# A sum of the first chunk's inverse on GpSimd, a copy on ScalarE, and a new order of all steps

## The chip, the core and the metric

The kernel runs on one core of one Trainium2 chip. A core has five engines with a queue each: TensorE (PE; its weight loads are shown as PEld), VectorE (DVE), ScalarE (ACT), GpSimd (POOL) and SyncE (SP, which here issues nearly all DMAs). Each works through its own queue in order and waits at semaphores for the others. The metric is the device time of one execution in microseconds (us), lower is better; it is given as the median of several executions.

## The reference

All is float32, but the two weights arrive as float64. First a linear recurrence with a 40x40 state for each of 4 x 8 heads over 768 time steps, then a two-layer perceptron on the 3072 tokens:

```python
for t in range(S):
    y[:, :, t] = np.einsum('bhd,bhde->bhe', rt, state)
    Sa = np.einsum('bhde,bhe->bhd', state, at)
    state_decay = state * wt[:, :, None, :] - np.einsum('bhd,bhe->bhde', Sa, bt)
    state = state_decay + np.einsum('bhd,bhe->bhde', vt, kt)
...
x = np.ascontiguousarray(attn_out.transpose(0, 2, 1, 3)).reshape(B * S, H * D)
h = x @ w_in
g = 0.5 * h * (1.0 + erf(h * inv_sqrt2))
return (g @ w_out).astype(np.float32)
```

Here B, H, S, D are 4, 8, 768, 40; `w_in` is 320x2048 and `w_out` 2048x320.

## The kernel before

The sequence is cut into 12 chunks of 64 steps. Within a chunk the recurrence becomes matrix products and the inverse of a triangular 64x64 matrix per head, which is built from 32x32 blocks; the chunks follow one another through the state. Behind each chunk its 256 tokens go through the perceptron, 8 steps `mh` for the first product, 4 `ge` for the activation, and for chunks 1 to 11 seven products `m1` to `m7` for the second (the first chunk uses four plain steps `pm`).

The program is a list of small functions, the steps. `order` (lines 19 to 111) returns one long string of tokens such as `mh.0.3`; line 1436 performs them in that order, and each step puts its instructions at the end of its engines' queues. No scheduler changes it: the order of the tokens is the order of every queue, and waits follow from who wrote and read which memory. The first number of a token is the chunk, or for the `c` steps a unit of the weights.

The steps that matter here:

- `sb` (L785) and `sk` (L790) scale b and k by the decays; `ta`, `tb`, `tk`, `tv`, `tr` (L752, L194) transpose on PE for chunks 0 to 2; `nm` and `nk` (L194, L865) give the triangular matrix N, `am`/`ak` and `vm`/`vk` two more such products.
- The inverse of chunk 0 goes by squaring: `qt` (L1001) transposes N, `qi` (L1008) adds the identity to N, `qi.0` for partitions 0 to 63 and `qi.1` for 64 to 127; a last letter `p` puts it on GpSimd, `v` on VectorE. `qm.0` to `qm.4` are the products on PE, `qz`, `qb`, `qa`, `qc`, `ql`, `qx` the work between them, `jm`, `jc`, `km`, `kt0`, `kt1` the last block.
- The inverses of chunks 1 to 11 go row by row on GpSimd: `iz`, then `ic.c.j0.j1` (L962, L964), 62 small instructions for a chunk. They need `nx` (L928) on VectorE, which needs `nd` (L923) on ScalarE and `nk`. `wx` (L933) takes the result.
- `av`, `xm` and the copies `xc0`, `xc1` (L1155) bring products into SBUF; `sm` applies the inverse, `sc` (L1176) masks; `pk` and `pb` give state and output, `om` and `od` scale them, `ox` moves parts of the output between partitions by eleven DMAs for each chunk, `ym` and `tn` use the turned state.
- The weights are loaded as raw words of float64 in 18 units (`Lf`, `Lf5` for `w_in`, units 0 to 9; `Ls` for `w_out`, units 10 to 17) and made into float32 by `cp`, `ce`, `cm`, `cs` (L607, L614, L621, L628) and then one of three ends: `cv` on VectorE (L636, L637), `cl`/`cn` on ScalarE with `cg` on GpSimd (L659, L660), or `cx` on PE with `cy`. The raw words lie in memory that later work needs: those of units 10 to 13 in `w_out_sb` itself, those of unit 15 in `gt`, the activations' tile, those of units 14 and 17 one after the other in `bk_rows`.
- `warm` are matmuls without use for the result. `parity_set` (a transpose on VectorE) reads what `stripes_set` on GpSimd wrote; `warm_first` needs `warm_set` on VectorE; `wT` and `cu` need `sums_mask` on GpSimd.
- PSUM is four banks. `take` (line 177) gives out the bank that has been free longest, `drop` returns it, both in the order of the tokens, so a product waits for the last reader of what lay in its bank.
- At the end `so.11.0` and four `sz` write the last rows; the last letter names the queue, `a` ScalarE's, `s` SP's.

Of the kernel before, what the change touches and what calls it, by code (L numbers as in the profile page):

```python
# [18 lines left out]
def order(chunks, first_seven):  # L19
    return """  # L20
        Lw.0 of_half_set warm_set pads_a.1 warm_first pads_a.0 stripes_set Lw.1 bias_set pads_rows.1 pads_VR.1
        sums_mask pads_w.0 pads_extra.3 La.0 pads_VR.0 identity pads_extra.0 first_ones.0 Lf.0.0.0 pads_w.1
# [8 lines left out]
        Lf5.0.1 ic.1.12.16 cp.7 ce.7 av.0 qa.4 cm.2 qx Ls.0 cm.7 cp.2 ql warm.4.21 ic.1.16.20 xc1.0 LV.1
        warm.4.13 ce.2 cs.7 xc0.0 cu.2 cv.7 jm.0 Lf5.0.0 sk.1.v warm.4.8 jc.0 cm.9 warm.4.22 pads_r.1 La.2 km.0
        ic.1.20.24 ec.2 warm.4.24 kt1.0 Lr.1 cs.2 kt0.0 warm.4.3 cv.2 sm.0 Lf.1.1.1 Ls.5 cp.9 warm.4.25
        ic.1.24.28 ce.9 cp.4 sc.0.1 ce.4 pk.0 Lb.2 sc.0.0 cs.9 tr.1 Lf.1.0.1 cm.4 cv.9 Lf.3.1.1 pb.0 rc.1
        unused.v Lf.3.0.1 ic.1.28.31 wT.2 om.0.0 tk.1 om.0.1 od.0.0 ox.0.0 od.0.1 tv.1 cs.4 oc.0 cv.4 ew.2 ta.2
# [10 lines left out]
        tn.1 lt.3 ym.2 wx.2 tb.3 pm.0.2 wb.2 yc.2 tc_.2 so.0.1 pw.3 ox.1.0 ew.3 jm.2 pc.0.0 unused.r xm.2 sa.3
        jc.2 wa.2.0 tr.3 km.2 xc0.2 Lk.3 mh.1.0 en.3 wa.2.1 La.4 sn.3 kt1.2 kt0.2 tv.3 nm.3 xc1.2 sk.3.p sm.2
        Lkt.3 nk.3 iz.3 nd.3 mh.1.4 nx.3 sc.2.0 ic.3.0.4 mh.1.5 sc.2.1 ta.4 pk.2 ge.1.2 ic.3.4.8 tk.3 pb.2 Lr.4
        kc.3 mh.1.2 oa.2.1 ws.0 Lbt.4 mh.1.6 ic.3.8.12 ws.1 od.2.1 mh.1.1 Lwt.4 oa.2.0 ws.2 mh.1.3 LV.3 od.2.0
        oc.2 tr.4 ge.1.0 mh.1.7 ws.3 Lw.4 ic.3.12.16 ot.2.0 om.2.0 vm.3 ge.1.3 am.3 ge.1.1 vk.3 so.0.0 m1.1  # L50
        ot.2.1 s1.1 om.2.1 m2.1 ak.3 ox.2.1 ic.3.16.20 tn.2 av.3 s2.1 e1.1 sb.3 ym.3 tb.4 m5.1 yc.3 Lkt.4 tw.4
        ic.3.20.24 m6.1 s3.1 lg.4 e2.1 ox.2.0 s4.1 lt.4 xm.3 pw.4 m3.1 Lb.4 ew.4 ic.3.24.28 xc1.3 m7.1 e3.1 en.4
        e4.1 La.5 tk.4 m4.1 e5.1 ic.3.28.31 Lr.5 sn.4 mh.2.4 e6.1 sa.4 so.1.1 wx.3 mh.2.5 kc.4 wb.3 LV.4 xc0.3
        tc_.3 cu.4 nm.4 Lv.4 ec.4 jm.3 sk.4.p nk.4 mh.2.2 ge.2.2 Lw.5 iz.4 nd.4 wa.3.0 nx.4 mh.2.3 jc.3 wa.3.1
        ic.4.0.4 ta.5 so.1.0 km.3 tv.4 ge.2.1 mh.2.0 Lbt.5 kt0.3 ic.4.4.8 kt1.3 lg.5 sm.3 Lwt.5 mh.2.1 sc.3.1
# [10 lines left out]
        xc0.5 xc1.5 kc.6 sa.6 m4.3 Lb.5 e5.3 vm.6 e6.3 so.3.1 nm.6 mh.4.6 nk.6 so.3.0 wx.5 La.7 wa.5.0 iz.6 tr.7
        mh.4.7 nd.6 wb.5 nx.6 tc_.5 ic.6.0.4 mh.4.2 Lwt.7 sb.5 vk.6 ge.4.3 am.6 ta.7 Lkt.7 jm.5 ic.6.4.8 ak.6
        mh.4.3 jc.5 Lbt.7 tw.7 mh.4.0 lt.7 ic.6.8.12 wa.5.1 LV.6 km.5 mh.4.1 kt0.5 Lv.7 kt1.5 ic.6.12.16 sm.5
        ge.4.0 ge.4.1 mh.4.4 sc.5.0 tb.7 ic.6.16.20 pk.5 sc.5.1 pw.7 cu.6 Lw.7 pb.5 mh.4.5 oa.5.0 oa.5.1
        ic.6.20.24 m1.4 om.5.0 ge.4.2 od.5.1 s1.4 m2.4 od.5.0 om.5.1 oc.5 s2.4 ox.5.1 m5.4 ic.6.24.28 s3.4 ew.7  # L70
        m6.4 s4.4 en.7 sa.7 m3.4 e3.4 sn.7 ot.5.0 La.8 ec.6 ot.5.1 m7.4 e1.4 tn.5 ic.6.28.31 ox.5.0 e2.4 m4.4
        e4.4 e5.4 sk.6.p nm.7 e6.4 wx.6 so.4.1 av.6 iz.7 tk.7 nk.7 so.4.0 mh.5.6 nd.7 Lb.6 nx.7 ym.6 ic.7.0.4
        tv.7 Lb.7 mh.5.7 yc.6 kc.7 Lwt.8 wa.6.0 mh.5.2 ic.7.4.8 ge.5.3 Lr.8 xm.6 vm.7 lg.7 xc1.6 wa.6.1 mh.5.3
        ic.7.8.12 vk.7 wb.6 xc0.6 ta.8 mh.5.0 sb.6 Lbt.8 tc_.6 jm.6 ic.7.12.16 am.7 LV.7 jc.6 km.6 ak.7 mh.5.1
        kt1.6 kt0.6 tb.8 ic.7.16.20 mh.5.4 tr.8 ge.5.0 tw.8 ge.5.1 sm.6 Lv.8 ic.7.20.24 mh.5.5 lt.8 sc.6.1 sc.6.0
# [1392 lines left out]
```

## Time and profile before

| what | us |
|---|---|
| median of three executions | 641.62 (640.03 to 642.96) |
| the profiled execution, its own time | 638.89 |
| its span, first to last instruction | 637.2 |
| PE busy in the span | 621.2 |
| VectorE busy | 463.5 |
| GpSimd busy | 383.5 |
| ScalarE busy | 311.6 |

The granted clock of PE averaged 0.994. DMA moved 64 MB at 101 GB/s in the mean, more than 150 GB/s in most of the first sixth of the span.

How to read it: an engine's busy time is the union of its instructions. A line of the timeline gives start, length, engine, line of the code, operation, what it writes and reads, and in brackets the idle time of the engine before it with what ended that. Most PE steps of the recurrence share the line L194 and are told apart by the names of their tiles; `mh` is L1308, `m1` to `m7` are L1347, `pm` is L1429.

### The profile page before, as it was taken

What the parts mean: (1) busy time and instruction counts of PE and PEld (TensorE: products, weight loads), DVE (VectorE), ACT (ScalarE), POOL (GpSimd) and SP (SyncE); (2) the same over time, 40 slices, a digit from 0 to 9 for tenths busy, and PEclk for the clock granted to TensorE, in tenths of its full rate; (3) what the DMA queues carried; (4) which work ended last, traced back from release to release, by engine and by line L of the source; (5) the groups of instructions that cost most, each with busy time, mean ns of one, the idle gap of its engine ahead of it and who ended that gap; (6) DMA issues with size and microseconds to landing.
All of it is one profiled execution on the core that took longest, in us unless ns stands there. A gap on an engine that the chain in (4) does not pass through costs nothing.

```text
span 637.2 us, 27873 instructions
## 1 busy us (share of the span) xinstructions
PE 621.2 (97%) x12424; PEld 548.8 (86%) x12424; DVE 463.5 (73%) x555; ACT 311.6 (49%) x441; POOL 383.5 (60%) x783
## 2 busy tenths in 40 slices
PE   7989999999999999999999999999999999999997
PEld 4676887678998998998988998998998998989996
DVE  1889989989986996986867887984964784833212
ACT  3566684582645454735546536437563275241010
POOL 4568779728867848818958718958918808810000
PEclk9899999999999999999999999999999999999999
DMA  9998587947576458268366466368344440210100
GB/s 152 168 172 162 121 180 160 175 96 123 95 144 114 85 105 149 41 121 143 66 104 116 92 113 123 70 116 153 72 87 96 84 85 4 42 25 3 37 6 21
DMA packets 246898, 64.06 MB, mean 101 GB/s; under 512 B 228380, under 2 KB 243644, under 8 KB 246780
## 3 DMA queue, kind: packets, MB, share of 16 engines
q1 hardware_dynamic: 246340, 62.01, 52.8%
q8 instruction: 97, 1.59, 1.1%
q10 hardware_dynamic: 440, 0.29, 0.2%
q14 instruction: 21, 0.17, 0.1%
HBM read 54.39 MB, written 3.93 MB: 92 GB/s over the span
## 4 chain that ended last, share of the span: by engine, by line
PE 83%; DVE 5%; POOL 3%; ACT 3%; SPq 2%; issue 2%; DMA 1%; DVEq 0%; POOLq 0%; ACTq 0%
PE bank L1308 31%; PE bank L1347 27%; PE bank L194 24%; POOL W L964 2%; POOL tmp L962 2%; DVE conv L628 1%; SPq L447 1%; DMA bk_rows<-in_b_dram 1%; PE bank L1429 1%; SPq L577 1%; DVE SM L1176 1%; DVE conv L636 1%; DMA w_out_sb<-in_moe_w_out_dram 1%; ACT conv L1264 1%; ACT conv L614 0%
## 5 line engine op out<-in xcount | busy, mean ns | idle before, releaser
L1308 PE MATMUL bank<-xt,w_in_sb 64*128 64x256 f32 x1920 | 221.7, 382 | 0.0
L962 POOL TENSOR_TENSOR tmp<-W,Nb 128x126 f32<-128x126 f32 (+22 forms) x341 | 162.4, 476 | 74.4 <-DVE Nb L928 49.0
L1308 PEld LDWEIGHTS bank<-xt,w_in_sb 64*128 64x128 f32 x1920 | 182.0, 187 | 23.2 <-issue 0.8
L964 POOL TENSOR_TENSOR W<-W,tmp 128x126 f32<-128x126 f32 (+22 forms) x341 | 170.7, 501 | 26.7
L1347 PE MATMUL bank<-w_out_sb,gt 128*128 128x160 f32 x704 | 101.1, 301 | 0.0
L1347 PEld LDWEIGHTS bank<-w_out_sb,gt 128*128 128x128 f32 x704 | 96.6, 190 | 2.5 <-issue 1.2
L1313 ACT ACTIVATE gt<-bank 128x1024 f32<-128x1024 f32 x48 | 48.6, 1025 | 85.5 <-PE bank L1308 80.9
L1264 ACT COPY conv<-st 32x128 f32<-32x128 f32 (+2 forms) x55 | 28.0, 509 | 39.5 <-DVE st L1258 31.6
L1176 DVE TENSOR_TENSOR SM<-bank,upper 128x832 f32<-128x832 f32 (+1 forms) x24 | 23.0, 985 | 22.0 <-PE bank L194 21.9
L1300 DVE TENSOR_TENSOR os<-os,bank 128x160 f32<-128x160 f32 x44 | 13.9, 316 | 24.5 <-PE bank L1347 18.2
L1347 PE MATMUL bank<-extra,conv 128*128 128x160 f32 x208 | 30.3, 300 | 0.0
L1300 DVE TENSOR_TENSOR conv<-gt 128x1024 f32<-128x1024 f32 x11 | 14.1, 1286 | 21.6 <-ACT gt L1313 21.6
L1347 PEld LDWEIGHTS bank<-extra,conv 128*128 128x128 f32 x208 | 28.9, 190 | 0.1
L1228 DVE TENSOR_TENSOR st<-bank,st 128x832 f32<-128x832 f32 (+1 forms) x22 | 20.9, 986 | 8.0 <-PE bank L194 8.0
L790 POOL TENSOR_TENSOR bk_rows<-bk_rows,part 128x640 f32<-128x640 f32 x9 | 15.0, 1666 | 19.3 <-DMA bk_rows<-in_k_dram 15.6
L947 POOL MEMSET W<- 128x512 f32 x11 | 5.8, 526 | 34.6 <-DVE Tt L933 34.6
L722 DVE TENSOR_TENSOR_SCAN kT<-spare,kT 128x256 f32<-128x256 f32 x36 | 25.5, 768 | 1.4 <-ACT kT L715 1.4
L1347 PE MATMUL bank<-extra,gt 128*128 128x160 f32 x176 | 25.8, 300 | 0.0
L1347 PEld LDWEIGHTS bank<-extra,gt 128*128 128x128 f32 x176 | 24.5, 190 | 0.1
L1313 ACT ACT_TABLE_LOAD x18 | 23.1, 1283 | 0.3
L1347 PE MATMUL bank<-extra,SM 128*128 128x160 f32 x144 | 21.2, 300 | 0.0
L194 PEld LDWEIGHTS bank<-SM,Tt 64*64 64x64 f32 x768 | 17.2, 133 | 4.1 <-issue 2.3
(218 smaller groups left out, 1113.9 us busy)
## 6 DMA issues: line engine op xcount, KB each, us to landing
bk_rows<-in_b_dram SPq DMA_DIRECT2D x24, 160.0 KB
bk_rows<-in_k_dram SPq DMA_DIRECT2D x24, 160.0 KB
out_dram<-os SPq DMA_DIRECT2D x46, 80.0 KB
VR<-in_v_dram SPq DMA_DIRECT2D x22, 160.0 KB
w_tile<-in_w_dram SPq DMA_DIRECT2D x36, 80.0 KB
a_pairs<-in_a_dram SPq DMA_DIRECT2D x18, 144.0 KB
v_pairs<-in_w_dram SPq DMA_DIRECT2D x18, 144.0 KB
v_pairs<-in_v_dram SPq DMA_DIRECT2D x18, 144.0 KB
```

The costliest lines, as they stand in the source:

```text
L194: nc.tensor.matmul(o, lhsT, rhs, start=first, stop=True, skip_group_check=True)
L722: nc.vector.tensor_tensor_scan(logs[:, at:at + n], onward, logs[:, at:at + n], 0.0, ALU.mult, ALU.add)
L790: (nc.vector if q == "v" else nc.gpsimd).tensor_tensor(to, rows(k_of(c)), decays(c), ALU.mult)
L962: nc.gpsimd.tensor_tensor(t, W[:, BL // 2 - rows:, rest:rest + 1].to_broadcast([P, rows, rest]), Nb[:, rest:rest + 1, :rest].to_broadcast( ...
L964: nc.gpsimd.tensor_tensor(own, own, t, ALU.add)
L1176: nc.vector.tensor_tensor(SM[:, g, :, :, cols], pair_of(f"S{c}_", g).rearrange("p x i c -> p i x c")[:, :, :, cols], kept, ALU.mult)
L1228: nc.vector.tensor_tensor(to, pair_of(f"QY{c}_", g)[:, :, :, cols], to, ALU.add)
L1264: nc.scalar.copy(apart.rearrange("p e i g d -> p (e i g) d")[to_rows, :, to_col:to_col + n], st.rearrange("p e i g c -> p (e i g) c")[rows ...
L1300: nc.vector.tensor_tensor(to, one_, other, how)
L1308: nc.tensor.matmul(ph[:, x, s], w_in_sb[half(x), kt, p * P:(p + 1) * P], xt[half(x), kt], start=kt == 0, stop=kt == NK - 1)
L1313: nc.scalar.activation(gt[:, 4 * q:4 * q + 4].rearrange("p (x s) t -> p x s t", x=2), bank(f"ph{c}_{q}").rearrange("p x (s t) -> p x s t", ...
L1347: nc.tensor.matmul(po[:, n, :DM // 2], l_[:, f], r_[:, f], start=f == 0, stop=f == NF // 2 - 1)
```

## The change

Two steps change engines. `qi.1.v` becomes `qi.1.p`: the second half of the identity sum of chunk 0 moves from VectorE to GpSimd (the short description calls it a part of the second chunk's set-up; the code shows that it belongs to the inverse of chunk 0). `xc1` of chunk 0 moves from VectorE to ScalarE:

```diff
     @step
     def xc1(c):
-        xcopy(c, 1, nc.scalar.copy if 0 < c < 3 else nc.vector.tensor_copy)
+        xcopy(c, 1, nc.scalar.copy if c < 3 else nc.vector.tensor_copy)
```

The rest is a new string of tokens. Beside `qi.1` its tokens differ from the old ones in two things. Seven `warm` tokens stand where 13 stood. The weight units that end on GpSimd (`cl`, `cn`, `cg`) are 4, 9, 15 and 17, where they were 0, 8, 14 and 17, and units 0, 8 and 14 end on VectorE (`cv`). All other tokens are the same ones in another place, in all chunks and on all queues, DMAs included. The beginning, and the part around the first chunk's second product, in the old and the new string:

```diff
-        Lw.0 of_half_set warm_set pads_a.1 warm_first pads_a.0 stripes_set Lw.1 bias_set pads_rows.1 pads_VR.1
-        sums_mask pads_w.0 pads_extra.3 La.0 pads_VR.0 identity pads_extra.0 first_ones.0 Lf.0.0.0 pads_w.1
-        Tt_zero warm.4.5 Lb.0 lg.0 onward_set pads_r.0 lg.1 wT.0 upper_mask Lf.1.1.0 first_ones.1 pads_extra.1
...
-        cn.14 cs.14 cg.14 am.2 cp.15 cm.15 ce.15 vm.2 Ls.14 mh.0.5 vk.2 ak.2 Ls.15 ic.2.16.20 pm.0.0 cs.15 Ls.13
-        cv.15 Ls.12 ge.0.3 ge.0.2 cm.17 Lk.4 ta.3 cn.17 sm.1 ic.2.20.24 tw.3 pm.0.1 lg.3 Lv.3 cp.16 cp.17 sc.1.1
...
+        pads_a.1 Lw.0 pads_extra.1 Tt_zero Lw.1 first_ones.1 pads_VR.0 first_ones.0 pads_w.0 stripes_set identity
+        parity_set warm_set pads_extra.2 Lb.0 warm_first iz.1 bias_set La.0 pads_a.0 of_half_set lg.0
+        pads_extra.0 pads_r.1 La.1 pads_extra.3 sums_mask lg.1 wT.0 pads_w.1 onward_set Lf.1.1.0 upper_mask cu.0
+        Lf.1.0.0 Lf.0.1.0 wT.1 ec.0 Lb.1 ew.0 sb.0 ew.1 tb.0 sn.0 Lf.0.0.0 ta.0 sa.0 Lf.2.1.0 nm.0 Lr.0 cu.1 cm.1
+        Lk.0 nk.0 cn.1 warm.4.27 ec.1 qt qi.0.p LV.0 qm.0 sb.1 ta.1 qi.1.p qc.0 cp.1 tb.1 sa.1 warm.4.13 sn.1
+        Lf.3.0.0 cm.0 qz.0 Lf.3.1.0 nm.1 cp.0 qb.0.1.a qb.0.0.v pads_r.0 ce.0 pads_VR.1 qm.1 nk.1 ce.1 Lf.0.1.1
+        cs.1 nd.1 tr.0 cl.1 nx.1 Lw.2 cx.1 qa.1 sk.0.p qz.1 qb.1.1.a cy.1 qc.1 Lf.0.0.1 ic.1.0.4 qb.1.0.v tk.0
...
+        mh.0.7 cm.15 Ls.13 cs.12 cl.15 cv.12 cn.15 Ls.12 km.1 wa.1.1 cs.15 cg.15 pm.0.0 Lw.3 kt1.1 ge.0.3 cp.14
+        cm.14 ce.14 ta.3 kt0.1 pads_rows.1 ic.2.24.28 ge.0.2 cs.14 sm.1 cv.14 pm.0.1 Ls.15 sc.1.0 Ls.14
+        ic.2.28.31 cp.16 sc.1.1 ce.16 Lbt.3 cm.16 cs.16 tk.2 cl.17 cm.17 pk.1 cp.17 Lr.3 cn.17 cv.16 ce.17 pb.1
+        cs.17 cg.17 pm.0.2 LV.3 oa.1.1 lg.3 oa.1.0 kc.2 om.1.1 om.1.0 od.1.1 ox.1.0 am.2 pc.0.0 od.1.0 cu.3 ak.2
```

The ends of the two strings:

```diff
-        e3.11 m4.11 e5.11 so.11.0 sz.11.0.1.a e6.11 sz.11.1.0.a sz.11.0.0.s sz.11.1.1.a
+        m6.11 e2.11 m3.11 e3.11 e4.11 m7.11 m4.11 e5.11 so.11.0 sz.11.1.1.a e6.11 sz.11.0.1.a sz.11.0.0.s
+        sz.11.1.0.a
```

More of the change, by code (lines that the diff above doesn't have):

```diff
@@ L31, in order @@
[L31 to L35, printed above, removed]
@@ L46, in order @@
[L46 to L50, printed above, removed]
@@ L51, in order @@
[L51 to L55, printed above, removed]
@@ L66, in order @@
[L66 to L70, printed above, removed]
@@ L71, in order @@
[L71 to L75, printed above, removed]
@@ new lines, in order @@
+        ak.0 jm.0 cl.9 cs.7 av.0 Ls.0 jc.0 cv.7 qx km.0 La.2 cs.2 ic.1.24.28 warm.4.1 cv.2 Lk.1 xc1.0 tv.1 kt1.0
+        xc0.0 Lb.2 cp.4 cm.4 kt0.0 cm.9 vc.1 cp.9 sm.0 ic.1.28.31 Ls.2 ce.4 ce.9 pk.0 sc.0.1 Lk.2 cn.9 cn.4
+        sc.0.0 Lf.1.1.1 pb.0 sk.1.v Lf.1.0.1 cs.9 cg.9 Lf.3.0.1 ta.2 om.0.0 om.0.1 wT.2 od.0.0 ox.0.0 od.0.1
+        unused.a tk.1 sb.2 ew.2 unused.v cs.4 tb.2 cl.4 sa.2 cg.4 sn.2 sk.2.v kc.1 wx.1 nm.2 ox.0.1 oc.0 am.1
+        nk.2 ot.0.0 vm.1 iz.2 cp.6 nd.2 cm.6 ce.6 nx.2 ot.0.1 mh.0.0 cs.6 ic.2.0.4 vk.1 cv.6 LV.2 tn.0 mh.0.1
@@ new lines, in order @@
+        oc.3 tw.5 ot.3.0 m5.2 s2.2 lt.5 ak.4 ot.3.1 ic.4.16.20 m2.2 Lkt.5 s4.2 m6.2 s3.2 ox.3.0 pw.5 m3.2 e3.2
+        e1.2 m7.2 e2.2 ew.5 ic.4.20.24 vk.4 La.6 e4.2 tn.3 av.4 e5.2 Lv.5 ym.4 tk.5 ic.4.24.28 m4.2 yc.4 Lb.5
+        en.5 xm.4 e6.2 so.2.1 sn.5 ic.4.28.31 mh.3.6 xc0.4 ta.6 sa.5 mh.3.7 tv.5 xc1.4 Lwt.6 cu.5 ge.3.3 wx.4
+        vm.5 tc_.4 iz.5 nm.5 kc.5 Lk.5 mh.3.2 ec.5 vk.5 nk.5 Lr.6 jm.4 nd.5 mh.3.3 nx.5 sk.5.p Lw.6 mh.3.0
+        ic.5.0.4 ge.3.1 wb.4 wa.4.0 am.5 Lbt.6 jc.4 wa.4.1 ic.5.4.8 km.4 ak.5 mh.3.1 kt0.4 so.2.0 kt1.4 tr.6 LV.5
@@ new lines, in order @@
+        wx.6 nm.7 yc.6 tc_.6 iz.7 so.4.1 xm.6 tk.7 La.8 mh.5.6 xc0.6 xc1.6 wa.6.0 kc.7 nk.7 Lr.8 mh.5.7 nd.7 nx.7
+        jm.6 Lb.7 ic.7.0.4 vm.7 jc.6 wb.6 am.7 vk.7 mh.5.0 tw.8 ge.5.3 ic.7.4.8 wa.6.1 ak.7 mh.5.4 lt.8 km.6
+        ic.7.8.12 mh.5.1 kt1.6 pw.8 kt0.6 sm.6 ge.5.0 mh.5.5 tr.8 ic.7.12.16 sc.6.1 sc.6.0 mh.5.2 ge.5.2 ta.8
+        sb.6 Lbt.8 mh.5.3 ic.7.16.20 pk.6 ge.5.1 s1.5 pb.6 LV.8 cu.7 s2.5 m5.5 Lk.8 ic.7.20.24 oa.6.1 ec.7 oa.6.0
+        Lkt.8 m1.5 om.6.0 od.6.1 om.6.1 m2.5 s4.5 ox.6.1 ic.7.24.28 od.6.0 m6.5 ew.8 s3.5 oc.6 sa.8 en.8 m3.5
@@ new lines, in order @@
+        tb.8 e1.5 Lv.8 ot.6.1 sn.8 m7.5 e3.5 sk.7.p ot.6.0 e2.5 e4.5 ox.6.0 tn.6 m4.5 ic.7.28.31 e5.5 av.7 e6.5
+        tk.8 so.5.1 ym.7 wx.7 mh.6.2 iz.8 tc_.7 yc.7 La.9 kc.8 sb.7 wb.7 mh.6.3 wa.7.0 tv.8 Lr.9 nm.8 ge.6.1 xm.7
+        Lwt.9 nk.8 mh.6.6 nd.8 xc1.7 wa.7.1 xc0.7 nx.8 so.5.0 mh.6.7 ic.8.0.4 tr.9 Lb.8 vm.8 ge.6.3 Lkt.9
+        ic.8.4.8 am.8 jm.7 ak.8 mh.6.4 Lw.8 jc.7 vk.8 ta.9 ic.8.8.12 mh.6.0 tw.9 Lbt.9 lt.9 km.7 mh.6.1 kt1.7
+        ic.8.12.16 pw.9 kt0.7 sm.7 ge.6.0 mh.6.5 sc.7.1 sc.7.0 lg.8 ic.8.16.20 tb.9 pk.7 ge.6.2 cu.8 Lw.9 pb.7
@@ new lines, in order @@
+        e5.8 mh.9.6 ic.10.28.31 ot.9.1 so.8.0 en.11 tn.9 e6.8 mh.9.2 sn.11 so.8.1 wx.10 Lv.11 sa.11 iz.11 mh.9.3
+        mh.9.7 ge.9.1 nm.11 ge.9.3 av.10 nk.11 ym.10 sb.10 nd.11 wa.10.0 mh.9.4 tc_.10 wb.10 nx.11 yc.10
+        ic.11.0.4 tv.11 mh.9.5 jm.10 ge.9.2 ic.11.4.8 xm.10 jc.10 wa.10.1 km.10 xc0.10 xc1.10 mh.9.0 kt1.10
+        ic.11.8.12 tk.11 kt0.10 cu.11 sm.10 mh.9.1 ec.11 sc.10.0 ic.11.12.16 sc.10.1 pk.10 ge.9.0 s1.9 pb.10 m1.9
+        oa.10.1 ic.11.16.20 om.10.1 kc.11 m2.9 oa.10.0 om.10.0 vm.11 e1.9 s2.9 ox.10.1 m5.9 s3.9 ic.11.20.24 s4.9
```

111 lines of the change are left out of this document (52 added, 59 removed).

## The prediction

> **What bounds the kernel now.** I first read the busy time by windows, cut at 135 us, to see where TensorE (PE) is short of work. Columns: the window, its length, then busy time with instructions of PE, PEld, DVE, ACT and POOL, granted clock, DMA share, GB/s.
>
> ```profile
> 0.00:135.00 135.00, 123.57 (x2654) 95.29 (x2657) 110.67 (x148) 82.07 (x112) 92.06 (x189) 0.97 0.82 155
> 135.00:640.00 505.00, 497.63 (x9777) 453.53 (x9776) 352.82 (x407) 229.57 (x330) 291.42 (x594) 1.00 0.46 85
> ```
>
> From 135 us to PE's last instruction at 632.6 us PE is busy for all 497.6 us. Both orders have the same matmuls after the step that ends there, so this stage is worth nothing unless the new order opens holes in it. The time is decided by when PE has done `pm.0.0` to `pm.0.3` and `ym.2`: at 134.94 us now (the start of `jm.2` in the timeline of PE). I call this the common point. Before it PE idles for 11.4 us and does 13 `warm` tokens of about 1.0 us each, which fill waits. VectorE is busy for 93 of the 100 us from 20 to 120 (the same windows in steps of 10 us), so the start is a chain through VectorE, with GpSimd's block inverses (`ic`) beside it.
>
> Then the timeline, for the places that the change touches (start, length, engine, line, out<-in; the bracket is the idle time before and what ended it):
>
> ```profile
> 13.40 0.82 DVE L785 SCALAR_TENSOR_TENSOR extra<-bk_rows,part 128x640 f32<-128x640 f32 x1 [11.94 <-DMA bk_rows<-in_b_dram]
> ...
> 20.33 0.42 DVE L621 TENSOR_SCALAR conv<-w_out_sb 128x512 uint32<-128x512 uint32 x1
> 20.66 1.48 DVE L607 TENSOR_SCALAR conv<-w_out_sb 128x512 uint16<-128x512 uint16 x1
> 22.07 1.23 DVE L1001 STREAM_TRANSPOSE st<-N 128x1024 f32<-128x1024 f32 x1
> ```
>
> ```profile
> 20.50 2.77 POOL L1008 TENSOR_TENSOR turned<-N,ident 32x512 f32<-32x512 f32 x2 [11.86 <-DVE N L865]
> ...
> 82.24 0.39 POOL L962 TENSOR_TENSOR tmp<-W,Nb 128x31 f32<-128x31 f32 x1 [1.59 <-DVE Nb L928]
> ...
> 104.77 1.81 POOL L659 TENSOR_TENSOR conv<-conv,bk_rows 128x640 f32<-128x640 f32 x1
> ```
>
> ```profile
> 109.79 1.94 ACT L1313 ACTIVATE gt<-bank 128x1024 f32<-128x1024 f32 x2 [4.43 <-DVE conv L636]
> ```
>
> ```profile
> 110.85 1.66 PE L194 MATMUL bank<-SM,Tt 64*64 64x104 f32 x64
> ```
>
> Seen here: VectorE waits for `b` until 13.40; `qt` (L1001) stands behind two conversions; `ic.2` begins when `nx.2` (L928) is done; and ScalarE's `ge.0.3` (L1313) waits until the words of weight unit 15, which lie in `gt`, have been read by the conversion.
>
> **The two moves.** `qi.1` leaves VectorE, where its two sums take 24.18 to 25.56: -1.37 us; on GpSimd they cost 2.7 (the two of `qi.0` took 2.77). `xc1.0` leaves VectorE at 0.98 and costs ScalarE about 0.84 (`xc0.0`, the same copy, took 0.83). VectorE has 2.35 us less ahead of everything. The `cg`/`cv` swaps (units 0, 8, 14 to VectorE; 4, 9, 15 to GpSimd) keep the same number of each kind; only their places count.
>
> **The start.** `Lb.0` moves from the fifth load to the third. Three loads of two times 160 KB at the 126 GB/s of the first ten-us window take 7.8 us after the first issue at 0.8, so `b` lands near 9 us instead of 13.3. But `parity_set` now leads VectorE's queue and needs `stripes_set`, which stands behind seven memsets on GpSimd (0.8 to 3.3 us by their rows): `warm_first` starts near 4.1 instead of 1.52, ends near 8.2 and, with `sums_mask` also later, `wT.0` starts at 8.4 (now 7.89). `cu.0` then ends at 10.9 and `ec.0` at 11.6, so `sb.0` starts at 11.6: -1.8. `tb.0` before `ta.0` gives back 0.6: `nk.0` at 18.0 (now 19.19). `qt` follows at once, at 19.2 (now 22.07).
>
> GpSimd does both `qi` from 19.3 to 24.8, under `qm.0`, `ta.1`, `tb.1` and `nm.1`; their reader `qm.1` comes at 26 to 27 (now 28.35), so they are hidden with 1 to 2 us to spare. The L607 row above took 1.48 beside `qi.0`, against 0.42 for the first row of that line (16.64): a conversion beside a GpSimd sum loses about 1.06. `sb.1`, `cp.1` and `cm.0` now lie beside four such sums. I charge 1.0 for it, bounds 0 and 2.7 (four sums of 1.35 that stop VectorE half of the time).
>
> [...]
>
> `nk.1` and `nx.1` now follow `qb.0` directly: `nx.1` ends near 31 (now 36.31), so `ic.1` runs 31 to 66 (now 36.46 to 72.56, 1.4 of it memsets). `cg.9`, two memset steps, `cg.4` and `iz.2` (2.5 + 2.2 + 2.5 + 1.3) fit before `ic.2`.
>
> **VectorE's queue.** Summing the rows that stand ahead of it in each order: 62.7 us after `sb.0` begins now, 54.7 in the new order (the moves, one conversion to GpSimd, and `vk.1`, `ak.1` and the last conversions of units 6 and 8 put behind it). Now 13.40 + 62.7 + 6.1 idle = 82.2. New: 11.6 + 54.7 + 6.1 + 1.5 for new waits in its queue (`sa.1` for `ta.1`, `qz.2` for `qm.2`) + 1.0 for the sums on GpSimd = 74.9. `ic.2` starts 7.3 us earlier than at 82.24.
>
> **The loss.** `mh.0.0` needs `xt`, whose eleven `ox.0` DMAs follow the last weight load on SP's queue (67.27 now, about 66.5 then, 7.9 us): 75.0, now 76.19. From there to the end of `pm.0.0` PE takes 34.7 us now; `tk.2` and `am.2` (1.0 each) go behind it: 75.0 + 32.7 = 107.7. Next is `sm.1`. It takes the PSUM bank that `ge.0.3` frees and needs `kt0.1`; ScalarE's new order is `ge.0.3`, `ce.14`, `kt0.1`. And `ge.0.3` now waits for `cg.15`, which GpSimd does after `ic.2.20.24`. That far `ic.2` takes 82.24 to 117.83 less `cg.14`'s 3.2 = 32.4 us beside VectorE's conversions, which lie beside it in the new order too. So `cg.15` starts at 74.9 + 32.5 = 107.4; its first sum (L659, 1.81) ends at 109.2; `ge.0.3` 1.0, `ce.14` 0.8, `kt0.1` 0.6: `sm.1` at 111.7, later than now (110.85). PE waits 4.0 us there, and VectorE's `cs.14`, queued behind `ce.14`, starts near 111 though VectorE could at 107: units 14 and 17 come late with it.
>
> From `sm.1` to the common point: 1.6 + `pm.0.1` 4.5 + `tk.2` 1.0 + `pk.1` 1.5 + `pb.1` 1.5 + `pm.0.2` 4.5 + `am.2` 1.0 + `cu.3` 0.6 + `pm.0.3` 4.4 + `av.2` 1.5 + `ym.2` 1.05 = 23.2. `pm.0.2` reads unit 17 near its end; `Ls.14` overwrites unit 14's words, so `cs.17` ends near 122 and `cg.17` near 126, and PE waits about 1.3 more. 111.7 + 23.2 + 1.3 = 136.2, +1.3. The next close call, `nm.3` behind `sa.3`: +0.2.
>
> **The tail.** One of ScalarE's three output DMAs reads what `e6` writes (L1300 at 632.67). In the old order it is the second and holds up the third; in the new order it is the last:
>
> ```profile
> 631.87 2.54 ACTq L1422 DMA_DIRECT2D out_dram<-os  x3
> 632.67 0.32 DVE L1300 TENSOR_TENSOR os<-os,bank 128x160 f32<-128x160 f32 x1 [0.83 <-PE bank L1347]
> 633.02 0.47 SPq L1422 DMA_DIRECT2D out_dram<-os  x1
> ```
>
> Three issues share 2.54 us, 0.85 each at most: -0.7, bounds 0 and -0.85.
>
> **Sum.** +1.3 + 0.2 - 0.7 = +0.8. The profiled execution took 638.89 (span 637.2 and 1.7 around it), so 639.7 for the same kind of execution; the median of the runs, 641.62, lies 2.7 above it: 642.4.
>
> **Rivals.**
> - *Faster*: GpSimd reaches `cg.15` before PE reaches `sm.1`. The smallest rows of each shape sum to 21.4 us for this part of `ic.2`, against 32.4; if it takes 28, `sm.1` starts at 107.7 and the waits behind shrink too: -4.0 and the tail, 641.6 - 4.7 = 637. For it: VectorE has 2.35 us less and starts 1.8 earlier, which is also 4.2; six `warm` tokens less. Against it: `ic.2` lies beside nearly the same conversions. 0.25.
> - *Slower*: the same chain, later. From `ge.0.3`'s release on nothing covers it: each us that `cg.15`'s first sum ends after 109.2 is a us of the time. It decides (over 0.5%, 3.2 us) from 111.6 on. [...] For it: the new order has many more close couplings, and each that I missed adds. Holes after 135 us would add likewise. 0.32.
> - *Forecast*, within 0.5% (about what a measurement can tell from no change): 0.43. Its own range is 639 to 645.5.
>
> That the moves are not made is no rival: the tokens and the engine choice say so plainly.
>
> The range reaches to both rivals: 636.5 to 648.
>
> **What would show it.** `sb.0` near 11.6; `ic.1` from about 31 and `ic.2` from about 75; ScalarE idle ahead of the first L1313 after 100 us, ended by POOL L659; a PE hole of about 4 us before the L194 `SM,Tt` group near 111; no PE idle after 137. The prediction is wrong if PE has no hole there (faster), or if `ic.2` starts after 77 or PE idles past 140 (slower).

## The result and the profile after

The changed kernel takes 647.15 us (median of 14 executions, 640.84 to 650.24), the kernel before 641.25 us beside it (14 executions, 640.03 to 644.03). The ratio is 1.0065, 95% interval 1.0043 to 1.0087: slower, by a little more than the 0.5% that was named as the bound of what can be told from no change. The medians themselves lie 5.9 us (0.9%) apart, more than this ratio says, because the median of the changed kernel falls into the longer of two groups of executions. A second measurement gave 1.0068 (1.0039 to 1.0096).

The profiled execution is the slowest of the 14: 650.24 us, span 648.1, mean granted clock 0.987. The 14 lie in two groups by that clock: eight at 0.989 or less take 646.7 to 650.2 us, six at 0.993 or more take 640.8 to 645.1. So the two profiled executions differ by more (10.9 us of span) than the kernels do, and the ledger below is made for these two executions first; the one of before is also shorter than any of the 14 beside the changed kernel.

Busy time by windows of the changed kernel. The second cut lies where `ym.2` ends, which is the common point in this order:

```profile
0.00:135.00 135.00, 116.17 (x2464) 91.11 (x2468) 100.21 (x136) 72.21 (x98) 93.80 (x189) 0.94 0.78 149
...
143.06:644.26 501.20, 499.46 (x9776) 454.23 (x9776) 352.25 (x407) 238.08 (x337) 291.73 (x593) 1.00 0.47 86
```

Two things are to be seen. In the first 135 us PE does 190 matmuls less than before (2464 for 2654), and the granted clock is 0.94 for 0.97; the common point comes at 143.06, 8.1 us later than 134.94. And the later part takes 501.2 us for 497.7; PE is busy for 499.46 of it, for 497.63 with the same products before. The predicted places, from the timeline of the changed kernel:

```profile
12.82 0.83 DVE L785 SCALAR_TENSOR_TENSOR extra<-bk_rows,part 128x640 f32<-128x640 f32 x1 [8.84 <-ACT part L743]
...
19.69 1.25 DVE L1001 STREAM_TRANSPOSE st<-N 128x1024 f32<-128x1024 f32 x1
19.74 5.80 POOL L1008 TENSOR_TENSOR turned<-N,ident 32x512 f32<-32x512 f32 x4 [10.57 <-DVE N L865]
...
81.54 0.52 POOL L962 TENSOR_TENSOR tmp<-W,Nb 128x31 f32<-128x31 f32 x1 [2.30 <-DVE Nb L928]
...
113.47 1.56 POOL L659 TENSOR_TENSOR conv<-conv,gt 128x640 f32<-128x640 f32 x1
115.06 1.02 ACT L1313 ACTIVATE gt<-bank 128x1024 f32<-128x1024 f32 x1 [5.38 <-POOL conv L659]
116.11 0.83 ACT L614 ACTIVATE conv<-conv,rebias 128x640 uint16<-128x640 uint16 x1
116.85 0.56 ACT L1117 COPY Tt<-bank 32x512 f32<-32x512 f32 x1
```

```profile
117.46 3.05 PE L194 MATMUL bank<-SM,Tt 64*64 64x104 f32 x64 [3.95 <-ACT Tt L1117]
120.44 5.57 PE L1429 MATMUL bank<-w_out_sb,gt 128*128 128x320 f32 x16
```

The chain is the one that was drawn: `cg.15` on GpSimd behind `ic.2` releases `ge.0.3`, `ce.14` and `kt0.1` follow on ScalarE, and PE waits 3.95 us for them ahead of `sm.1`. But `ic.2` begins at 81.54 and not at 74.9, and the two PE steps behind the hole take 3.05 and 5.57 us, for 1.66 and 4.57 in the profile of before. PE was also late at the hole already: it had done `pm.0.0` at 113.51, where 107.7 was forecast.

The end of the span, with the last write of `os` issued from ScalarE's queue:

```profile
643.43 1.86 ACTq L1422 DMA_DIRECT2D out_dram<-os  x3
644.29 0.32 DVE L1300 TENSOR_TENSOR os<-os,bank 128x160 f32<-128x160 f32 x1 [0.90 <-PE bank L1347]
644.64 0.47 SPq L1422 DMA_DIRECT2D out_dram<-os  x1
```

The three issues end at 645.29, not 1.8 but 1.0 us after PE's last matmul: from there to the end of the span it is 3.89 us for 4.54.

**The ledger of the two profiled executions.** Common point +8.1, later part +3.5, end -0.65: +10.9. Of the +8.1, 2.7 stand ahead of the hole (`pm.0.0` ends at 113.51, for 110.85), 3.95 are the hole, and 1.5 the stretch from `sm.1` to the common point (25.6 us for 24.1).

### The profile page after: what moved, and what is told of

Its sections match the earlier page's. It is cut to its first block, busy times and chain, and to the rows that moved or that the text cites. A ratio compares the mean times of both kernels' runs of the same rounds, so it can differ in the third digit from the quotient of the medians.

```text
span 648.1 us, 27872 instructions
## 1 busy us (share of the span) xinstructions
PE 623.7 (96%) x12412; PEld 551.3 (85%) x12412; DVE 459.7 (71%) x552; ACT 316.7 (49%) x445; POOL 386.4 (60%) x785
## 3 DMA queue, kind: packets, MB, share of 16 engines
q8 instruction: 97, 1.59, 1.1%
## 4 chain that ended last, share of the span: by engine, by line
PE 83%; SPq 3%; DMA 1%; ACT 1%; issue 1%; DVE 0%; POOL 0%
PE bank L1308 32%; PE bank L1347 26%; PE bank L194 22%; PE bank L1429 2%; SPq L455 1%; SPq L1249 1%; SPq L577 1%; DVE os L1300 0%; DMA xt<-xt 0%; DMA w_tile<-in_w_dram 0%; SPq L1246 0%; POOL conv L659 0%; SPq L447 0%; ACT gt L1313 0%; ACT late L837 0%
## 5 line engine op out<-in xcount | busy, mean ns | idle before, releaser
L962 POOL TENSOR_TENSOR tmp<-W,Nb 128x126 f32<-128x126 f32 (+22 forms) x341 | 160.1, 469 | 90.9 <-DVE Nb L928 65.4
L194 PEld LDWEIGHTS bank<-SM,Tt 64*64 64x64 f32 x768 | 18.5, 141 | 7.5 <-ACT Tt L1117 4.5
L194 PE MATMUL bank<-SM,Tt 64*64 64x104 f32 (+1 forms) x768 | 20.8, 260 | 4.0 <-ACT Tt L1117 4.0
L790 POOL TENSOR_TENSOR bk_rows<-bk_rows,part 128x640 f32<-128x640 f32 x9 | 15.8, 1759 | 10.9 <-DMA bk_rows<-in_k_dram 10.9
```

The lines of the kernel that those rows point to most:

```text
L194: nc.tensor.matmul(o, lhsT, rhs, start=first, stop=True, skip_group_check=True)
L790: (nc.vector if q == "v" else nc.gpsimd).tensor_tensor(to, rows(k_of(c)), decays(c), ALU.mult)
L962: nc.gpsimd.tensor_tensor(t, W[:, BL // 2 - rows:, rest:rest + 1].to_broadcast([P, rows, rest]), Nb[:, rest:rest + 1, :rest].to_broadcast( ...
```

## Experiments

All ratios are to the kernel before, run on the same chip between the others. Theory 1 was that the new order loses the time, by the hole of 3.95 us ahead of `sm.1` and the low granted clock behind it (0.57 from 115 to 120 us); the rivals are named in each expectation.

**The two moves alone.**

```diff
-        ... qi.1.v ...
+        ... qi.1.p ...
-        xcopy(c, 1, nc.scalar.copy if 0 < c < 3 else nc.vector.tensor_copy)
+        xcopy(c, 1, nc.scalar.copy if c < 3 else nc.vector.tensor_copy)
```

> The old order with the two moves alone (the second sum of qi on GpSimd, xc1 of chunk 0 on ScalarE, each at its old place). Theory 1, the new order makes the loss and the moves are harmless: VectorE is 2.35 us shorter ahead of sc.0.1, but sm.0 (its products end at 60.0) gates sc.0.1, so at most 1.2 us reach ic.2 and the ratio to before is 0.997 to 1.001. Theory 2, the moves cost by themselves (GpSimd sums beside VectorE, a longer ScalarE queue ahead of kt0.0): 1.003 or more, and VectorE's instructions beside the four sums lose over 1.4 us.

Measured: 642.19 us, ratio 0.9994 (0.9970 to 1.0018). From `sb.0` to `nx.2` VectorE works 61.5 us for 62.7 and waits 7.7 for 6.1; `ic.2` begins at 82.35 for 82.24. The moves are harmless, and of no use in the old order: what VectorE no longer does, it waits. This profile shows one thing more, to which the account below comes back: PE idles for 2.81 us ahead of `pm.0.0`, and the granted clock (the third number from the end) stays at 1.00.

```profile
109.55 4.57 PE L1429 MATMUL bank<-w_out_sb,gt 128*128 128x320 f32 x16 [2.81 <-DVE VR L865]
```

```profile
105.00:110.00 5.00, 2.19 (x20) 1.57 (x17) 5.00 (x5) 0.83 (x1) 3.95 (x6) 1.00 0.71 167
```

**The new order without the moves.**

```diff
-        ... qi.1.p ...
+        ... qi.1.v ...
-        xcopy(c, 1, nc.scalar.copy if c < 3 else nc.vector.tensor_copy)
+        xcopy(c, 1, nc.scalar.copy if 0 < c < 3 else nc.vector.tensor_copy)
```

> The new order with both moves undone (the second sum of qi on VectorE, xc1 of chunk 0 on VectorE). Theory 1, the order makes the loss: within 2 us of the changed kernel, 1.004 to 1.011 of before, with the hole ahead of sm.1 still at 3 us or more. Theory 2, the moves make it: 1.002 or less of before.

Measured: 645.02 us, ratio 1.0052 (1.0027 to 1.0076). The order makes the loss. Its profiled execution was a quick one, and the hole in it is 0.5 us, not over 3:

```profile
108.59 2.14 POOL L659 TENSOR_TENSOR conv<-conv,gt 128x640 f32<-128x640 f32 x1
...
110.76 1.02 ACT L1313 ACTIVATE gt<-bank 128x1024 f32<-128x1024 f32 x1 [1.88 <-POOL conv L659]
...
113.16 1.66 PE L194 MATMUL bank<-SM,Tt 64*64 64x104 f32 x64 [0.48 <-ACT Tt L1117]
```

The sum ends at 110.73 and `sm.1` starts 2.43 us later, as in the changed kernel (115.03 and 117.46). `pm.0.0` had just ended (112.68), since `mh.0.0` began late. Behind this short hole `sm.1` takes 1.66 us, and the common point comes 23.2 us after its start.

**Unit 15 ended sooner**, so that the hole goes:

```diff
-        ... ic.2.20.24 Lwt.3 ... cs.12 cl.15 cv.12 cn.15 Ls.12 km.1 wa.1.1 cs.15 cg.15 pm.0.0
+        ... Lwt.3 ... cs.12 cl.15 cn.15 cs.15 cv.12 Ls.12 km.1 wa.1.1 cg.15 ic.2.20.24 pm.0.0
-        ... ge.0.3 cp.14 cm.14 ce.14 ta.3 kt0.1 ...
+        ... ge.0.3 kt0.1 cp.14 cm.14 ce.14 ta.3 ...
```

> The changed kernel with unit 15 ended sooner: cs.15 and cn.15 ahead of cv.12, cg.15 ahead of ic.2.20.24, and kt0.1 ahead of ce.14. Theory 1, the hole of 4 us at sm.1 is a loss that nothing covers, and the low granted clock behind it (sm.1 3.05 instead of 1.66, pm.0.1 5.57 instead of 4.57) is its consequence: the hole is under 1 us, sm.1 and pm.0.1 take 1.7 and 4.6, the time is 4 to 6.5 us below that of the changed kernel, 0.996 to 1.001 of before. Theory 2, the step behind (cg.17, cs.14, nm.3) is as late anyway: under 2 us gained, 1.003 or more.

Measured: 644.70 us, ratio 1.0042 (1.0017 to 1.0067), some 1.5 us below the changed kernel by the ratios, with intervals that overlap. The number is that of theory 2 (under 2 us gained, 1.003 or more); what theory 1 said of the place itself is also seen. Timeline of PE, around the place (the order string is one line shorter here, so every line number is one lower):

```profile
108.92 1.66 PE L193 MATMUL bank<-SM,Tt 64*64 64x104 f32 x64
110.50 4.58 PE L1428 MATMUL bank<-w_out_sb,gt 128*128 128x320 f32 x16
...
118.90 3.50 PE L1428 MATMUL bank<-w_out_sb,gt 128*128 128x320 f32 x12
124.37 1.34 PE L1428 MATMUL bank<-w_out_sb,gt 128*128 128x320 f32 x4 [1.98 <-POOL w_out_sb L659]
```

No hole ahead of `sm.1`, and a granted clock of 1.00 from 105 to 125 us. But now PE waits 1.98 us inside `pm.0.2` for unit 17 (`cg.17`), which the hole had covered: the second wait that the prediction named takes part of the place of the first, as theory 2 had it.

**The hole filled.** Twelve products without use between `pm.0.0` and `sm.1`; they write columns of the bank of `pm` that no step reads:

```diff
+    @step
+    def fill(i):
+        for j in range(12):
+            mm(bank("po0")[:, 1, 3 * P:], ident, cum_m)
...
-        ... kt0.1 pads_rows.1 ic.2.24.28 ...
+        ... kt0.1 fill.0 pads_rows.1 ic.2.24.28 ...
```

> The changed kernel with twelve products without use (3.2 us at 0.27 each) put on TensorE between pm.0.0 and sm.1; they write columns of the bank of pm that no step reads. Theory 1, the idle hole lowers the granted clock for what follows: with the hole filled sm.1 takes 1.7 and pm.0.1 4.6 us, granted clock 1.00 from 115 to 125, and the time is 1 to 2.5 us below that of the changed kernel. Theory 2, the low clock there is not from the hole: sm.1 and pm.0.1 stay at 3.0 and 5.6, and the time is that of the changed kernel or up to 1 us above it.

Measured: 648.75 us (6 executions), ratio 1.0096 (1.0073 to 1.0119). Locally theory 1 holds. The windows around the hole, of the changed kernel and then of this one (the columns as above, the granted clock third from the end):

```profile
110.00:115.00 5.00, 3.51 (x14) 2.13 (x12) 2.81 (x4) 0.00 (x0) 4.61 (x7) 1.00 0.74 172
115.00:120.00 5.00, 2.54 (x60) 2.54 (x64) 2.58 (x3) 3.23 (x4) 4.61 (x9) 0.57 0.08 15
120.00:125.00 5.00, 5.00 (x25) 3.41 (x21) 4.23 (x7) 1.50 (x2) 3.49 (x10) 0.75 0.96 224
```

```profile
110.00:115.00 5.00, 3.89 (x33) 3.38 (x35) 1.53 (x2) 2.50 (x4) 4.69 (x9) 1.00 0.11 19
115.00:120.00 5.00, 5.00 (x77) 3.90 (x77) 4.97 (x8) 1.56 (x2) 4.29 (x10) 1.00 0.44 125
120.00:125.00 5.00, 5.00 (x141) 4.35 (x140) 4.54 (x6) 4.06 (x5) 3.31 (x5) 1.00 1.14 203
```

With products in the hole the clock stays at 1.00, `sm.1` takes 1.66 and `pm.0.1` 4.58 us, and the common point comes 23.2 us after the start of `sm.1`, for 25.6 in the changed kernel. Yet the time did not fall: in the profiled execution the later part takes 505.4 us, with six stalls of another kind (see the last section), 2.7 us together; the other half of what it lost against the rest of these profiles is open. The time is above both theories; whether the stalls are in every execution of this kernel is not shown by one profile.

**The changed kernel once more.**

> The changed kernel once more, for its spread and a second profile on the chip of the three runs beside it. Both theories: 1.004 to 1.009 of before. Theory 1 (TensorE idles more early on, and each stretch of low granted clock that follows delays the chain): executions at a mean granted clock of 0.995 or more lie 3 us or more below those at 0.989 or less. Theory 2 (the clock has no part): no such step between them.

Measured: 646.49 us (9 executions), 1.0068 (1.0039 to 1.0096). Two executions at 0.995 take 643.1 and 646.7 us, the two at 0.989 or less 647.3 and 649.2: the step is there in the mean, but the groups are not as far apart as expected, and four executions are few. In this profile `ic.2` begins at 79.04, the first sum of `cg.15` ends at 112.35, `sm.1` starts at 114.78 after a hole of 3.8, and the common point is 140.78.

**Fewer warm products in the old order.**

```diff
-        mm(pt[:, 0, :n * P], ident, cum_m.unsqueeze(1).to_broadcast([P, n, P]))
+        if n: mm(pt[:, 0, :n * P], ident, cum_m.unsqueeze(1).to_broadcast([P, n, P]))
...
-        warm.4.5   (and 8, 22, 3, 25, 23)
+        warm.0.5
```

> The kernel before with six of its 13 warm tokens emptied (they still take and return their bank, but issue no product): as many as the changed kernel has. Theory 1, fewer warm products cost by the granted clock: mean granted clock of the executions 0.991 or less (0.993 now), 1.002 to 1.006 of before. Theory 2, they are harmless or in the way: 0.997 to 1.001.

Measured: 642.56 us, ratio 1.0014 (0.9987 to 1.0042), between the two expectations. The mean clock of the executions falls from 0.9932 to 0.9878, as theory 1 had it, but the time stays within what can be measured. Inside this run, though, a lower clock goes with a longer time: the six executions at 0.987 or less take 641.7 to 647.1 us, the six above it 640.1 to 642.6. Whether the clock makes the time long, or the waits that make it long also lower the clock, this run does not tell.

**Longer warm products in the new order.**

```diff
-        mm(pt[:, 0, :n * P], ident, cum_m.unsqueeze(1).to_broadcast([P, n, P]))
+        for z in range(n // 4): mm(pt[:, z, :4 * P], ident, cum_m.unsqueeze(1).to_broadcast([P, 4, P]))
...
-        warm.4.27   (and 13, 12)
+        warm.8.27
```

> The changed kernel with three warm tokens (27, 13, 12, each ahead of an idle time of TensorE) twice as long: 3.1 us more of products without use. Theory 1: the stretches of low clock near 30 and 55 us go, qm.1 and jm.0 take 2.1 and 1.2 us, ic.2 starts at 78 or sooner, and the time is 2 to 4 us below that of the changed kernel beside it. Theory 2: no stretch goes, and the time is the same or up to 1.3 us above it (0.5 and 0.75 us of delay at qm.0 and nm.1).

Measured: 644.53 us, ratio 1.0054 (1.0029 to 1.0078). In the profile the low clock near 55 us is gone (1.00 from 50 to 60 us, where the changed kernel has 0.50 from 54.22 to 61.05; `jm.0` takes 1.20 us for 1.92) and `ic.2` begins at 78.63; the stall in `qm.1` remains (1.2 us). The mean clock is 0.9946 for 0.9921. By ratios the gain is 0.9 us, less than the 2 to 4 us of theory 1, and the intervals overlap: not settled.

**Two warm products less in the new order.**

```diff
-        warm.4.12   (and 19)
+        warm.0.12
```

> The changed kernel with warm tokens 12 and 19 emptied; they stand ahead of jm.0 and wait for ScalarE's rc.1 and ec.2, the readers of their banks. Theory 1a, what costs is that they stand in the way: jm.0 starts as soon as ql ends (near 55.0 instead of 56.75) and the time falls by 1 to 2 us. Theory 1b, what costs is the clock: TensorE idles 3 us ahead of jm.0, its clock falls, jm.0, av.0 and km.0 take 1.9, 2.8 and 2.4, and the time is the same or up to 2 us above the changed kernel beside it.

Measured: 645.40 us, ratio 1.0068 (1.0040 to 1.0097): no change. Both halves are seen in the profile: `jm.0` starts at 51.2, as soon as `ql` lets it, after 3.1 us of idle time, and then runs at a granted clock of 0.50 (50 to 55 us) and takes 1.92 us. What one gives, the other takes.

**The new order up to the common point, then the old one**, with the new end:

```diff
-        (after ym.2: the remaining steps as in the new order)
+        (after ym.2: the remaining steps as in the old order, with the new end)
```

> The new order with both moves up to ym.2, then the remaining steps in the old order, with only the four last writes of the output as in the new one. Theory 1, the new order loses about 2 us in its later part too (nm.7 waits for a PSUM bank, and many small gaps): from the end of ym.2 to TensorE's last instruction 497.7 to 498.6 us instead of 499.7 to 501.2, no wait for os (L1300) ahead of nm.7, and 1.002 to 1.005 of before. Theory 2, all of the loss is in the first 143 us and the later part only carries it: 499.7 or more there, and 1.005 or more.

Measured: 648.88 us (6 executions), ratio 1.0134 (1.0100 to 1.0167). That is far above theory 1, and theory 2 covers the number but not the reason: joining the two orders made a wait of its own. It shows the price of a hole better than the kernel that it was to explain:

```profile
139.38 0.74 PE L194 MATMUL bank<-turned,N 32*32 32x32 f32 x64 [2.23 <-DVE turned L1068]
140.05 3.05 PE L194 MATMUL bank<-st,aT 40*64 40x104 f32 x64
...
145.16 4.64 PE L1308 MATMUL bank<-xt,w_in_sb 64*128 64x256 f32 x20
```

```profile
140.00:150.00 10.00, 9.13 (x170) 7.29 (x161) 4.99 (x5) 5.36 (x9) 0.91 (x1) 0.50 0.95 152
```

PE is idle for 2.23 us, and then the granted clock is 0.50 for ten us: `xm.2`, `km.2` and `mh.1.0` take 2.98, 2.13 and 4.57 us from start to start, for 1.59, 0.68 and 2.36 in the kernel before, 5.1 us more (0.9 of it a stall of its own in `km.2`). Without those steps and the wait the later part is that of the old order to within 1.1 us, and `nm.7` has no wait, as theory 1 had it.

**The same with unit 15 ended sooner** (the edit shown above).

> The same with unit 15 ended sooner (as in the earlier run: cs.15 and cn.15 ahead of cv.12, cg.15 ahead of ic.2.20.24, kt0.1 ahead of ce.14). Theory 1, the hole at sm.1 and the later part are the whole of the loss: 0.998 to 1.002 of before, no idle time ahead of sm.1 over 1 us. Theory 2, something else in the head costs as much again (the inverse of chunk 0 with its slow stretches, the later xt): 1.003 or more.

Measured: 647.58 us (6 executions), ratio 1.0109 (1.0082 to 1.0135). No hole ahead of `sm.1`, 1.25 us of waiting for unit 17, and the same wait at the seam (2.2 us at `jm.2`; the profiled execution has a mean granted clock of 0.981), so that the time can't decide between the theories. Against the run before it some 1.6 us are gained by the ratios, as in the new order itself; here too the intervals overlap.

**The old order up to `jm.2`, then the new one.**

```diff
-        (after jm.2: the remaining steps as in the old order)
+        (after jm.2: the remaining steps as in the new order, with its end)
```

> The old order up to jm.2, then the remaining steps in the new order, with its end. Theory 1, the later part of the new order costs 2.0 us and its end gives back 0.65: from the start of jm.2 to TensorE's last instruction 499.5 to 500.5 us (497.7 before), the end 3.9 us (4.54 before), 1.001 to 1.004 of before. Theory 2, the later part is harmless in itself: 497.7 to 498.6 us, and 0.997 to 1.000 of before.

Measured: 645.77 us (6 executions), ratio 1.0095 (1.0069 to 1.0122). `jm.2` starts at 135.20, as before, so all of the loss is behind it: 503.2 us for 497.7, with waits of 0.39, 0.64, 1.02 and 0.46 us at `mh.1.6`, `m4.1`, `km.3` and `nm.7`. The new later part is not harmless in itself; its size here is above both expectations and is not that in the changed kernel, since the PSUM banks (the four tiles `bank0` to `bank3` of the code) stand in another rotation behind the joint.

**The moves and the new end in the old order.**

```diff
-        ... sz.11.0.1.a e6.11 sz.11.1.0.a sz.11.0.0.s sz.11.1.1.a
+        ... sz.11.1.1.a e6.11 sz.11.0.1.a sz.11.0.0.s sz.11.1.0.a
```

> The old order with the two moves and the four last writes of the output as in the new order. Theory 1: the end (TensorE's last instruction to the end of the span) 3.9 us instead of 4.54, the moves harmless, 0.996 to 1.000 of before. Theory 2, the end's gain is lost elsewhere: 4.5 us or 1.001 and more.

Measured: 640.42 us, ratio 1.0007 (0.9987 to 1.0026). From PE's last matmul to the end it is 3.92 us for 4.54, as in every kernel with the new end (3.8 to 4.0), but 0.6 us is below what the times can tell. No kernel tried here beats the one before by more than the interval.

## Why the prediction was right and where it was wrong

The time, 647.15 us, lies in the range of 636.5 to 648.0, at its upper end, beside the price of the rival *slower* (647.5). The likeliest case, +0.8 us and within 0.5%, fell short: the kernel is 0.65% slower. By the prediction's own signs it is the rival *slower* that came: in the profiled execution `ic.2` starts after 77 and PE idles past 140. That its price was met so closely is luck. It lay 5.1 us above the 642.4, made of 1.7 for GpSimd's sums (their upper bound of 2.7 less the 1.0 charged) and 3.4 for a slow `ic.2` (in the profile of before `ic.6.20.24` took 7.5 us where `ic.2`'s took 4.1). Neither came, since VectorE worked 1.5 us less than charged and `ic.2` was 0.6 quicker than forecast. That four sums stop VectorE for half of their time, as the bound has it, was the author's estimate and no run shows it; measured was VectorE's work from `sb.0` to `nx.2`, 54.2 us in the changed kernel, for 55.7 with the charge, and 61.5 with the moves alone, for 62.7 before. What came in their place are terms that the prediction had small or not at all.

**What held.** The place of the hole and the chain that ends it. PE waits 3.95 us ahead of `sm.1`, for 4.0. In six profiles with `cg.15` at its place in the changed order, and in that of the new order without the moves, `sm.1` starts 2.42 or 2.43 us after the first sum of `cg.15` ends, for 2.4 in the prediction (1.0 + 0.8 + 0.6). `ic.2` takes 31.9 us up to `ic.2.20.24`, for 32.5. VectorE's work from `sb.0` to `nx.2` is 54.2 us in the profiled execution, for 55.7 with the charge. From `sm.1` to the common point it is 23.2 us where the granted clock stays at 1.00 (the filled hole), for 23.2. `nx.1` ends at 31.07, for 31, and GpSimd's second `qi` is hidden, as forecast. The end gains 0.65, for 0.7. And the rival's rule, that each us of `cg.15`'s first sum after 109.2 is a us of the time, is exact as far as `sm.1`: the sum ended at 115.03, 5.8 later, and `sm.1` started at 117.46, 5.8 later than 111.7.

**What failed.** The first step is "1.5 for new waits in its queue". From `sb.0` to `nx.2` VectorE waits 14.4 us in the profiled execution, 8.3 more than before. It works less, and waits instead: the inverse of chunk 0 is a chain through PE, ScalarE and VectorE, and VectorE, with less to do between its turns, stands there. Its longest wait, 2.39 us at 35.54, is for a product of `cx.1` that stood on PE behind a stall in `qm.1`. The end of the chain, in the timeline of the changed kernel, ScalarE first and then VectorE:

```profile
58.77 1.18 ACT L1089 COPY turned<-bank 32x512 f32<-32x512 f32 x2 [2.91 <-PE bank L194]
59.97 2.50 ACT L1060 COPY Tt<-turned 32x512 f32<-32x512 f32 x4
62.48 1.62 ACT L1155 COPY SM<-bank 128x832 f32<-128x832 f32 x2
...
62.59 0.69 DVE L1114 COPY Tt<-bank 32x512 f32<-32x512 f32 x1 [2.11 <-PE bank L194]
...
67.22 1.96 DVE L1176 TENSOR_TENSOR SM<-bank,upper 128x832 f32<-128x832 f32 x2 [2.34 <-PE bank L194]
```

`jc.0` waits for `jm.0` on PE, then `qx`, `xc1.0`, `xc0.0` and `kt0.0` stand in one row on ScalarE; VectorE, with nothing else in its queue, waits 2.11 and 2.34 us. The moved copy lies in this row, not beside it. The sum for the profiled execution: `sb.0` 1.2 late (`warm_first` took 5.49 us, for 4.25 before), work -1.5, waits +6.8 on the 7.6 that were charged, so `ic.2` starts 6.6 late and `sm.1`, after -0.6 in `ic.2` and -0.25 in the sum itself, 5.8. Over the eight profiles that have the new head and both moves, VectorE waits 8.6 to 14.4 us and `ic.2` starts between 76.2 and 81.5: even the quickest is 1.3 later than forecast.

The same chain made PE late by another way, which the prediction had at 75.0. The first of the `ox.0` DMAs that bring `xt` was to follow the last weight load on SP's queue, at 66.5. That load's issue ended at 66.74, but SP's queue then waited until 72.55 for `om.0` on VectorE (L1234, which ended at 72.51), behind the inverse:

```profile
72.60 0.90 SPq L1246 DMA_DIRECT2D xt<-xt  x1
```

So `mh.0.0` began at 79.25 and waited 0.88 us more for the rest of `xt`, and PE ended `pm.0.0` 5.8 later than forecast. Ending `cg.15` sooner can't bring that back.

How much of these waits is always there and how much is chance of an execution is not settled. Three sources are seen: the order on ScalarE (above); a stall of 1.0 to 1.4 us inside `qm.1`, in most of these profiles; and half speed of PE around `qm.1` or `jm.0` (a granted clock of 0.50 from 30.33 to 33.74 and from 54.22 to 61.05 us in the changed kernel). The runs with more or fewer warm products moved the time by less than can be told. Since the executions of the changed kernel at the lower clock take the longer times, the stretches at half speed may be much of the spread; that is argued, and not shown.

The second failed step is "From `sm.1` to the common point ... 23.2 + 1.3". The 1.3 for `cg.17` was not paid, since the hole itself gave `cg.17` the time. In its place stands the low clock behind the hole, which the prediction did not have at all: in the profiles with the new head, with a hole of 2.3 to 4.0 us the stretch takes 24.8 to 26.0 us in five profiles, with a hole of 0.5 or a filled one 23.2. So 136.2 + 5.8 + 2.4 - 1.3 = 143.1, and the common point was measured at 143.06.

The clock records show stretches at 0.50 of 3.41, 6.83 or 10.24 us ahead of PE's last instruction, so one, two or three times 3.41: 3.41 from 30.33 us, 6.83 from 54.22 and 6.83 from 115.66 in the changed kernel, 6.83 from 14.63 in the profile of before, and 10.24 behind the 2.23 us without a matmul where the old order follows the new. The length of a hole alone does not decide: behind 1.98 us (unit 15 ended sooner, window 120 to 125 us) and 2.81 us (the two moves alone, window 105 to 110 us) the clock was 1.00, and the sixteen products of `pm` behind the second took 4.57 us, for 5.57 behind the hole in the changed kernel. In the profiled execution of the changed kernel the stretch runs from 115.66 to 122.48, so 5.0 us of it lie behind the hole, and they cost 2.4 us.

The third failed step is "no PE idle after 137". The change of all the steps behind the common point was costed at 0.2 (`nm.3`), and that wait did not come. In six of the seven profiles with the new later part in its own rotation of the banks (all but that of the filled hole) `nm.7` waits:

```profile
334.51 1.16 PE L194 MATMUL bank<-aT,nT 40*64 40x64 f32 x64 [0.69 <-DVE os L1300]
```

`nm.7` now follows `e6.4`, takes the bank that this step frees, and waits 0.64 to 0.70 us for it (in the old order `nm.7` stood ahead of `e6.4`). With it the later part takes 499.8 to 501.2 us in these six, for 497.7 to 498.8 in four profiles of the old one. `m4.1` accounts for up to 0.2, a stall of 0.6 to 0.9 in four of the six for more; some 1.2 us remain. They do not show as idle time, since PE's busy time itself is longer (499.46 us for 497.63), and their cause is open.

**The shares.** For an ordinary execution (4.2 us by the ratio): the later part some 2 us, the end -0.65, and the head the rest, some 3 us: the late chain of chunk 0 and the hole with its slow stretch. Some 1.5 us came back when unit 15 was ended sooner, by ratios whose intervals overlap. That the order makes the loss is shown; this division rests on the profiles, since the two runs that joined the orders made waits of their own and could not confirm it. The two moves in the short description have no part that can be measured in either order.

## What to carry to other kernels

The instructions taken from the busy VectorE were worth nothing here (with the moves alone 1.2 us less work and 1.6 us more waiting), since it waited for the same chain a few steps on; when an instruction is moved, count what it will wait for next, and look whether the engine that takes the work stands in that chain. A hole on TensorE can cost more than its length: here the granted clock was 0.50 for 10.24 us behind one of 2.23 us and for 6.83 us across the end of one of 3.95 us, though 1.00 behind one of 2.81 us, so price it with that and look at the granted clock in windows of 5 us. When such a hole is to be closed, look first whether TensorE itself would come any sooner: here it was late by the same chain. When an order of a whole program is made anew, the stages that were not meant need a sum of their own: here the part that the prediction costed at 0.2 us lost two.

## What was not expected of the hardware

Idle times of PE that the profile marks as "issue" stand at fixed places of the instruction stream. Two of them in the changed kernel:

```profile
30.23 1.49 PE L194 MATMUL bank<-turned,st 64*64 64x64 f32 x22 [1.40 <-issue]
...
344.15 0.47 PE L194 MATMUL bank<-rT,late 40*64 40x64 f32 x17 [0.92 <-issue]
```

Counted from the first matmul, such stalls lie ahead of matmul 349, 476, 855, 1239, 1366, 1494, 2765, 6843, 6972 and 8759 in the profiles of these kernels, close to whole multiples of 127.5 apart, each matmul having a weight load of its own (12412 of each in the changed kernel); a given place stalls in some executions (0.25 to 2.25 us) and not in others. One of 0.36 us, ahead of matmul 376 in the old order joined to the new, stands apart from these places. The kernel before has one, 1.08 us ahead of matmul 1494. In the kernel with the hole filled, 24 matmuls more than the changed kernel, they lie behind the filled hole at 3274, 6078, 7992, 8757 and 10671, again multiples of 127.5 apart, but ahead of other steps (its line numbers are five higher):

```profile
299.55 0.70 PE L1313 MATMUL bank<-xt,w_in_sb 64*128 64x256 f32 x4 [0.65 <-issue]
```

So with 24 matmuls more other steps stalled, and these stalls may be part of the spread of 4 to 9 us between executions of one kernel; that is an estimate from their lengths. The profile's list of DMA queues has one whose kind is "instruction", in the changed kernel as in the one before:

```profile
q8 instruction: 97, 1.59, 1.1%
```

Its 97 packets hold 16384 bytes each, one for every 255.9 of the 24824 matmuls and weight loads in the profile. In the packed traces each of the 38 stalls of at least 0.25 us in the fourteen profiles, the one at 376 too, ends 1.29 to 1.98 us after such a packet has landed: the 1.40 us above end at 30.23, and the packet landed at 28.26. At the other places the packet landed 1.37 us or more ahead of the matmul, in half of them over 4 us. The spacing agrees: 127.5 matmuls with their weight loads are 255 instructions. That PE stands there because its next instructions came late is the author's reading of these times and of the queue's name; no run changed the packets to show it. Why a place stalls in one execution and not in another is open.
